# The last three microseconds of a decode block: the output in two transfers from two engines, and wd in parts of six, four and two chunks

## The chip, the cores and the metric

The kernel runs on one core of one Trainium2 chip. The metric is the device time of that core in microseconds (us), the median of several runs. The experiments ran on three chips of the same kind, each beside the kernel before on the same chip. Besides the time, each run has a profile of one execution. Where the profile's own views are too coarse, I read two more records from the same trace: the start of every DMA packet, and the moment of every semaphore increment by a DMA ("landing").

## The reference, cut to what matters

One token for each of four sequences passes through an attention block and a feed-forward block. Nearly all bytes are the key and value caches; the change concerns only the end, where the feed-forward block's down projection is multiplied and the result stored.

```python
def setup_inputs():
    B, Sq, D = 4, 1, 640
    Hq, Hkv, Sk, Dh = 32, 32, 4096, 192      # k_cache and v_cache: [4, 32, 4096, 192] bf16
    ...                                      # w_gate, w_up: [640, 1536]; w_down: [1536, 640]

def reference(A_x, A_k_cache, A_v_cache, A_wq, A_wo, B_x, B_w_gate, B_w_up, B_w_down):
    ...
    def _B_ref(x, w_gate, w_up, w_down):
        g = _silu(x @ w_gate)
        u = x @ w_up
        return (g * u) @ w_down

    x = A_x
    h = x + _A_ref(_layernorm(x, axis=-1), A_k_cache, A_v_cache, A_wq, A_wo)
    h2 = h + _B_ref(_layernorm(h, axis=-1), B_w_gate, B_w_up, B_w_down)
    return h2                                # [4, 1, 640] bf16: 5 KB
```

## The kernel before

All loads but that of the 5 KB input are issued by SyncE, in the order in which they are needed; w_down ("wd") is the last, in three parts. It is used as `CF` = 12 chunks of 128 rows. Each chunk is four matmuls, one for each quarter of the 640 columns, and a chunk waits for the part that holds it.

```python
    wd_land = {}
    for lo, hi in ((0, 6), (6, 11), (11, CF)):
        t = dma("sp", lambda e, lo=lo, hi=hi: e.dma_start(
            wdsb[:, lo:hi, :], wd[:, :].rearrange("(q c) n -> q c n", c=CF)[:, lo:hi, :]), sem(f"s_wd{lo}"), k_free)
        for c in range(lo, hi):
            wd_land[c] = t
    # ... attention, layer norm, gate and up projections ...
    for c in range(CF):
        for n in range(4):
            a = op("pe", lambda e, c=c, n=n: e.matmul(
                psH[32 * n:32 * n + 32, 0:DQ], lhsT=guT[:, c, :], rhs=wdsb[:, c, n * DQ:(n + 1) * DQ],
                start=False, stop=(c == CF - 1), skip_group_check=True), [gut, wd_land[c], ln2])
    a = op("dve", lambda e: e.tensor_copy(out=outsb[:, 0:DQ], in_=psH[:, 0:DQ]), [a])
    fin = dma("act", lambda e: e.dma_start(
        out[:, 0, :].rearrange("b (n d) -> n b d", n=4),
outsb[0:128:RB, 0:DQ]), S_out, [a])
```

The result lies on 16 of the 128 partitions: quarter n of the columns of sequence b is on partition 32n + 8b, 160 values of bf16 (320 bytes). The store therefore moves 16 rows of 320 bytes in a pattern of 4 x 4 rows. ScalarE issues it, waits for the semaphore `S_out`, and ends the program.

## Time and profile before

| | before |
|---|---|
| time, median of 3 runs before the prediction | 990.47 us (990.11 to 990.52) |
| span of the profiled execution | 988.4 us |
| mean DMA rate over the span | 429 GB/s |
| PE busy, DVE busy | 59%, 56% |
| last landing of wd | 985.08 us |
| start of the cast that produces the output | 985.79 us |
| start of the output's issue; its last landing | 986.14 us; 987.90 us |

From the page of before: the busy time of each engine, the rate in 40 slices, and the count of packets by size.

```profile
span 988.4 us, 9461 instructions
PE 580.1 (59%) x4409; PEld 129.6 (13%) x2941; DVE 552.5 (56%) x447; ACT 117.1 (12%) x376; POOL 3.6 (0%) x18
DMA  9999999999999999999999999999999999999997
GB/s 403 426 440 432 430 438 424 440 430 434 438 424 442 430 432 438 424 442 430 434 436 426 440 434 430 438 426 438 434 430 438 426 438 434 430 438 426 438 431 325
DMA packets 10571, 424.39 MB, mean 429 GB/s; under 512 B 1220, under 2 KB 1348, under 8 KB 1732
```

In 39 of 40 slices the DMA engines are at 90% or more. The loads bound the kernel, and only what follows the last load, in the last slice, can be shortened by a change at the end.

From the chain of work that ended last, its last three steps in order of time (start us, length, what; "issue" steps of 0.02 to 0.04 us between them left out):

```profile
946.58 38.12 DMA wd_sb<-in_B_w_down_dram
984.75 1.02 PE pb L573 x18
985.79 0.33 DVE gu L576
```

The first of them is the second part of wd, which landed at 946.58 + 38.12 = 984.70 us; the last six chunks and the cast follow from it. Here is the timeline of the end, without a line of weight loads (start us, length, engine, line, operation, out<-in, count, and in brackets the idle time before and what ended it):

```profile
982.93 0.99 PE L573 MATMUL pb<-wd_sb,guT 128*32 128x160 bf16 x24 [1.62 <-DVE guT L569]
984.74 0.67 PEld L573 LDWEIGHTS pb<-wd_sb,guT 128*32 128x32 bf16 x24 [1.15 <-DMA wd_sb<-in_B_w_down_dram]
984.75 0.99 PE L573 MATMUL pb<-wd_sb,guT 128*32 128x160 bf16 x24 [0.83 <-DMA wd_sb<-in_B_w_down_dram]
985.79 0.33 DVE L576 CAST gu<-pb 128x160 bf16<-128x160 f32 x1 [2.91 <-PE pb L573]
986.14 1.13 ACTq L577 DMA_DIRECT2D out_dram<-gu  x1
```

The first six chunks (24 matmuls) run as soon as their input is there. Then PE waits 0.83 us for the second part and runs the last six chunks without a break: the third part, one chunk, landed before its chunk's first matmul started at 985.38 us. After the cast, the issue on ScalarE is recorded with 1.13 us.

### The profile page before, as it was taken

Reading aid. Unit: us, or ns where it says so; the run is one execution under the profiler, and the core shown is the slowest. Engines: PE = TensorE matmul, PEld = TensorE weight load, DVE = VectorE, ACT = ScalarE, POOL = GpSimd, SP = SyncE. Lnnn points to the kernel's source line nnn. Section 1 sums busy time; section 2 is a strip of 40 time slices with the busy share of each in tenths; the row PEclk is TensorE's granted clock in tenths of the full one; section 3 lists DMA queues with packets and bytes.
Section 4 is the critical chain, followed back from the end, with each engine's and each line's share of the span. In section 5 each row is a group of like instructions: output and inputs, shape, how many; then the busy total and the mean of one; then the engine's idle time right before and its main releaser. Section 6 shows DMA issues by size and latency. Waiting matters only on the chain.

```text
span 988.4 us, 9461 instructions
## 1 busy us (share of the span) xinstructions
PE 580.1 (59%) x4409; PEld 129.6 (13%) x2941; DVE 552.5 (56%) x447; ACT 117.1 (12%) x376; POOL 3.6 (0%) x18
## 2 busy tenths in 40 slices
PE   1677555666555576555557755656665555765554
PEld 0011011110101111001111110111101011110023
DVE  1486555566645556664556665555666455566621
ACT  0311111110111110011111011111101111100120
POOL 1000000000000000000000000000000000000000
PEclk9898777887777888777788777788877778887775
DMA  9999999999999999999999999999999999999997
GB/s 403 426 440 432 430 438 424 440 430 434 438 424 442 430 432 438 424 442 430 434 436 426 440 434 430 438 426 438 434 430 438 426 438 434 430 438 426 438 431 325
DMA packets 10571, 424.39 MB, mean 429 GB/s; under 512 B 1220, under 2 KB 1348, under 8 KB 1732
## 3 DMA queue, kind: packets, MB, share of 16 engines
q1 hardware_dynamic: 10512, 424.28, 99.5%
q8 instruction: 5, 0.08, 0.0%
q10 hardware_dynamic: 52, 0.01, 0.0%
q14 instruction: 2, 0.02, 0.0%
HBM read 424.29 MB, written 0.01 MB: 429 GB/s over the span
## 4 chain that ended last, share of the span: by engine, by line
DMA 67%; PE 18%; DVE 12%; issue 1%; SPq 1%; DVEq 0%
DMA k<-in_A_k_cache_dram 63%; DVE prod L413 12%; PE pb L161 12%; PE pb L463 4%; DMA wd_sb<-in_B_w_down_dram 4%; PE pb L421 2%; SPq L366 0%; DVE sc L426 0%; PE pb L469 0%; DVEq L413 0%; PE pb L573 0%; SPq L386 0%; SPq L392 0%; PE pb L435 0%; SPq L331 0%
## 5 line engine op out<-in xcount | busy, mean ns | idle before, releaser
L413 DVE TENSOR_TENSOR prod<-k,qball 128x6144 f16<-128x6144 bf16 x128 | 426.3, 3352 | 220.7 <-DMA k<-in_A_k_cache_dram 220.7
L161 PE MATMUL pb<-prod,identH 128*128 128x512 f16 x1408 | 385.0, 430 | 0.0
L421 PE MATMUL pb<-prod,identH 128*128 128x512 f16 x128 | 57.9, 452 | 339.5 <-DVE prod L413 339.5
L426 DVE TENSOR_REDUCE sc<-pb 128x32 f32<-128x512 f32 x128 | 88.0, 688 | 107.6 <-PE pb L161 107.6
L478 ACT ACTIVATE otmp<-pb,minv 128x192 f32<-128x192 f32 x32 | 13.5, 421 | 650.8 <-PE pb L463 650.8
L421 PEld LDWEIGHTS pb<-prod,identH 128*128 128x128 f16 x128 | 13.2, 103 | 586.2 <-DVE prod L413 481.3
L463 PE MATMUL pb<-v,pbuf 128*8 128x384 bf16 x1984 | 86.0, 326 | 0.0
L454 ACT ACTIVATE pbuf<-sc,negM 32x128 bf16<-32x128 f32 x128 | 73.4, 574 | 4.9
L463 PEld LDWEIGHTS pb<-v,pbuf 128*8 128x8 bf16 x1984 | 45.4, 86 | 28.8
L482 DVE SCALAR_TENSOR_TENSOR orow<-pb,minv,otmp 128x192 f32<-128x192 f32 x32 | 13.4, 418 | 55.0 <-ACT otmp L478 55.0
L498 PEld LDWEIGHTS pb<-orow,here 128*128 128x128 f32 x256 | 33.5, 191 | 73.8 <-issue 71.1
L498 PE MATMUL pb<-orow,here 128*128 128x48 f32 x256 | 31.7, 267 | 1.1 <-DVE orow L482 1.1
L454 ACT ACTIVATION_READ_ACCUMULATOR pbuf<-sc,negM 32x1 f32 x128 | 31.8, 248 | 0.0
L448 ACT ACTIVATE negM<-pb 128x4 f32<-128x4 f32 x32 | 5.6, 174 | 160.9 <-PE pb L444 160.9
L469 PEld LDWEIGHTS pb<-lsb,headm 128*128 128x128 f32 x64 | 12.3, 194 | 74.8 <-issue 71.1
L444 PE MATMUL pb<-negMc,ones_row 1*128 1x4 f32 x64 | 12.2, 258 | 11.9 <-DVE negMc L439 11.9
L435 PE MATMUL pb<-identF,msb 128*1 128x128 f32 x64 | 12.1, 271 | 9.8 <-DVE msb L431 9.8
L439 DVE TENSOR_REDUCE negMc<-pb 1x4 f32<-1x128 f32 x32 | 8.9, 279 | 15.1 <-PE pb L435 15.1
L444 PEld LDWEIGHTS pb<-negMc,ones_row 1*128 1x128 f32 x64 | 9.4, 182 | 21.3 <-DVE negMc L439 21.3
L469 PE MATMUL pb<-lsb,headm 128*128 128x1 f32 x64 | 9.2, 213 | 2.7 <-ACT pbuf L454 2.7
L491 ACT ACTIVATE here<-place 128x131 f32 (+1 forms) x32 | 10.0, 312 | 0.9
L431 DVE TENSOR_REDUCE msb<-sc 128x1 f32<-128x128 f32 x32 | 9.2, 286 | 1.1
(65 smaller groups left out, 85.1 us busy)
## 6 DMA issues: line engine op xcount, KB each, us to landing
k<-in_A_k_cache_dram SPq DMA_DIRECT2D x32, 6144.0 KB, 39.5
v<-in_A_v_cache_dram SPq DMA_DIRECT2D x31, 6144.0 KB, 25.5
wq_sb<-in_A_wq_dram SPq DMA_DIRECT2D x1, 7680.0 KB, 21.4
k<-in_A_v_cache_dram SPq DMA_DIRECT2D x1, 6144.0 KB, 39.2
wo_sb<-in_A_wo_dram SPq DMA_DIRECT2D x1, 5760.0 KB, 24.9
wo_sb<-in_A_wo_dram SPq DMA_DIRECT2D x1, 1920.0 KB, 26.9
wg_sb<-in_B_w_gate_dram SPq DMA_DIRECT2D x1, 1920.0 KB, 31.1
wu_sb<-in_B_w_up_dram SPq DMA_DIRECT2D x1, 1152.0 KB, 33.4
```

The lines of the kernel that those rows point to most:

```text
L161: return e.add_instruction(mybir.InstMatmult(name=e.bass.get_next_instruction_name(), engine=mybir.EngineType.PE, start_tensor_calc=start, ...
L413: op("dve", lambda e: e.tensor_tensor(out=prod[BUF[k]][:, :, :], in0=kslot[u % 2][:, k * QT:(k + 1) * QT, :], in1=qball[:, bass.ds(u + pr. ...
L421: op("pe", lambda e, j=j: (e.matmul if j == 0 else partial(held_matmul, e))(psR[k][:, 0:QT * R], lhsT=identH[:, :], rhs=prod[BUF[k]][:, :, ...
L426: op("dve", lambda e: e.tensor_reduce(sc[u % 2][:, k * QT:(k + 1) * QT], psR[k][:, 0:QT * R].rearrange("q (t r) -> q t r", r=R), AX.X, ALU ...
L435: op("pe", lambda e: e.matmul(psS[0:1, XT], lhsT=msb[:, 0:1], rhs=identF[:, :], start=True, stop=True), [g("rmax", u), g("negM", u - 1), p ...
L444: op("pe", lambda e: e.matmul(psS[:, XB], lhsT=ones_row[0:1, :], rhs=negMc[0:1, :], start=True, stop=True), [g("hmax", u), g("negM", u - 1 ...
L454: op("act", lambda e, h=h, r=r: e.activation(out=pbuf[r, :, h], in_=sc[u % 2][r, :], func=ACTF.Exp, bias=negM[r, h:h + 1], scale=alpha, ac ...
L463: op("pe", lambda e, t=t, n=n: e.matmul(psO[32 * n:32 * n + 8, 0:2 * DH], lhsT=pbuf[:, t:t + 2, :].rearrange("q t m -> q (t m)"), rhs=vsrc ...
L469: op("pe", lambda e: e.matmul(psS[:, XL], lhsT=headm[:, :, :].rearrange("q r m -> q (r m)"), rhs=lsb[:, :], start=True, stop=True), [g("ex ...
L478: op("act", lambda e: e.activation(out=otmp[:, :], in_=psO[:, 0:DH], func=ACTF.Copy, scale=minv[:, 0:1]), [g("pv", u), g("minv", u), g("st ...
L482: op("dve", lambda e: e.scalar_tensor_tensor(out=orow[:, :], in0=psO[:, DH:2 * DH], scalar=minv[:, 1:2], in1=otmp[:, :], op0=ALU.mult, op1 ...
L498: op("pe", lambda e, i=i: e.matmul(psT[:, bass.ds(JW * at_unit(u)[0], JW)], lhsT=here[:, NI - 1 - i:NI - 1 - i + 128], rhs=orow[:, JW * i: ...
```

## The change

Its intent is twofold. The second part of wd gets smaller, so that it lands earlier, and the third larger. The output's 16 rows go out in two transfers of eight, issued side by side by SyncE and ScalarE, so that each engine has less to issue.

```diff
-    for lo, hi in ((0, 6), (6, 11), (11, CF)):
+    for lo, hi in ((0, 6), (6, 10), (10, CF)):
...
-    fin = dma("act", lambda e: e.dma_start(
-        out[:, 0, :].rearrange("b (n d) -> n b d", n=4),
-outsb[0:128:RB, 0:DQ]), S_out, [a])
+    fin = [dma(eng, lambda e, n=n: e.dma_start(
+        out[:, 0, n * DQ:(n + 2) * DQ].rearrange("b (n d) -> n b d", n=2),
+        outsb[32 * n:32 * n + 64:RB, 0:DQ]), S_out, [a]) for n, eng in ((0, "sp"), (2, "act"))]
...
-        pr.emit(block, "act", [fin])
+        pr.emit(block, "act", fin[-1:])
```

The last wait is for the second token, whose value on `S_out` counts both transfers, so the program still ends after both.

## The prediction

> **What bounds the kernel now.** The loads. The page's slices show the DMA engines at 90% or more in 39 of 40 slices (mean 429 GB/s), while PE is busy 59% and DVE 56% of the 988.4 us span. The chain that ended last gives DMA 67%. The change touches only the last 4 us.
>
> **The end, from the timeline.** The DMA traffic thins out from 982.8 us and ends at 984.6 (windows of 0.1 us: share 1.16 at 982.9, about 0.2 from 984.0, 0 after 984.7): a few engines finish about 1.5 us after the others. The down projection runs its first six chunks at 982.93 (0.99 us), waits 0.83 us for the second part of wd (issued 946.58, landed 38.12 us later, 984.70), and runs the last six from 984.75 in 0.99 us. The third part (160 KB) landed near 985.05, before its chunk was reached, so it held nothing up. Then come the cast (985.79, 0.33 us) and the output's issue on ScalarE (986.14, 1.13 us); the output's bytes move at 987.40 to 987.55; the span ends at 988.4.
>
> **Part one, wd in 6, 4, 2.** The second part ends one chunk earlier. A lagging engine moves its 10 KB of a chunk in about 0.38 us (27 GB/s, an estimate from the windows), so chunks 6 to 9 should start near 984.35, end by 985.0, and the last two wait briefly for the third part (985.05, unmoved) and run 0.33 us. The cast moves from 985.79 to about 985.5: 0.25 us won. Packets under 2 KB should fall from 1348 to 1220, as 128 pieces of 1280 B become 2560 B.
>
> **Part two, two output transfers.** "DMA: Bandwidth & Descriptors" of the Trainium skill (Issuing engines are not separate DMA queues) says that issuing from several engines saves only sequencer time. That is what matters here: the issue of 16 rows in a 4x4x160 pattern took 1.13 us, against 0.40 us for the input's 16 rows in one plain pattern. If the excess is per row (about 45 ns, an estimate), eight rows cost about 0.77 us on each engine, side by side. Against it: the same page (Why a DMA increments its semaphore by 16 and not by 1) says that a transfer uses a number of engines that divides its slowest dimension, so the pieces share two engines instead of four. The output occupies about 0.34 engine-us in the windows; doubled per engine this costs about 0.09 us. If the excess is a fixed cost of the pattern, nothing is won. Weighing both, 0.2 us won.
>
> PE and DVE instructions are unchanged in order and number, so the loop should not move.
>
> **Sum.** 990.47 - 0.25 - 0.2 = 990.0 us, 0.05% faster, all on the chain. The repeats span 0.4 us, so it may barely show. Range 989.4 to 990.6. Faster by over 2%: 0.003; within 2%: 0.994; slower by over 2%: 0.003.
>
> **What would show it.** Right: the last 24 matmuls split in 16 and 8, the 16 starting 0.3 to 0.4 us earlier after guT; a wait under 0.2 us before the last eight; the two issues at the same moment, each 0.7 to 0.9 us; cast's end to span's end (2.28 us now) about 2.1. Wrong: issues near 1.1 us each, or one delayed by the other; the third part landing later than 985.1.
>
> **What would make it wrong.** The imbalance of the DMA engines at the end may differ by 0.5 us between runs and swallow the gain. SyncE may react later than ScalarE. [...]

## The result, and the profile after

| | before | after |
|---|---|---|
| time, median of 6 runs | 990.52 us (990.11 to 990.92) | 990.43 us (990.17 to 990.64) |
| ratio | | 0.9999, 95% interval 0.9986 to 1.0012 |
| span of the profiled execution | 988.4 us | 988.4 us |

A ratio here and below is the mean time of one kernel's fast runs over the mean of the other's in the same rounds, so it is not quite the ratio of the medians quoted. The time is the same within noise, and the interval is 2.6 us wide. Both parts of the change are far below that, so the time alone cannot say what they did. The traces can: their durations at the end repeat to a few hundredths of a microsecond from run to run, as the table of the experiments will show.

The page and the end of the chain of after:

```profile
span 988.4 us, 9462 instructions
DMA packets 10571, 424.39 MB, mean 429 GB/s; under 512 B 1220, under 2 KB 1220, under 8 KB 1732
947.66 37.35 DMA wd_sb<-in_B_w_down_dram
985.06 0.48 PE pb L573 x6
985.57 0.33 DVE gu L576
```

The packets between 512 bytes and 2 KB are gone, as predicted (128 pieces of 1280 bytes became 2560 bytes). The chain now runs through the third part of wd, landed at 947.66 + 37.35 = 985.01 us, and the last eight matmuls after it (0.48 us). The timeline of after:

```profile
982.80 0.99 PE L573 MATMUL pb<-wd_sb,guT 128*32 128x160 bf16 x24 [1.65 <-DVE guT L569]
984.28 0.40 PEld L573 LDWEIGHTS pb<-wd_sb,guT 128*32 128x32 bf16 x16 [0.81 <-DMA wd_sb<-in_B_w_down_dram]
984.28 1.24 PE L573 MATMUL pb<-wd_sb,guT 128*32 128x160 bf16 x24 [0.49 <-DMA wd_sb<-in_B_w_down_dram]
985.06 0.14 PEld L573 LDWEIGHTS pb<-wd_sb,guT 128*32 128x32 bf16 x8 [0.38 <-DMA wd_sb<-in_B_w_down_dram]
985.57 0.33 DVE L576 CAST gu<-pb 128x160 bf16<-128x160 f32 x1 [2.86 <-PE pb L573]
985.92 0.68 SPq L577 DMA_DIRECT2D out_dram<-gu  x1
985.92 1.38 ACTq L577 DMA_DIRECT2D out_dram<-gu  x1
```

Two things are to be seen. The last six chunks start 0.47 us earlier than before (984.28 against 984.75), then stop in the middle: the weight loads idle 0.38 us and go on when the third part has landed. The cast starts 0.22 us earlier. And the two issues do start together, but they are not alike: SyncE's is recorded with 0.68 us, ScalarE's with 1.38 us, longer than the 1.13 us that ScalarE took for twice the rows.

The windows show when the output's bytes moved (stretch, its length, busy time of each engine, clock, DMA share, GB/s). Before:

```profile
987.10:987.30 0.20, 0.00 (x0) 0.00 (x0) 0.00 (x0) 0.00 (x0) 0.00 (x0) 0.50 0.00 0
987.30:987.43 0.13, 0.00 (x0) 0.00 (x0) 0.00 (x0) 0.00 (x0) 0.00 (x0) 0.50 0.00 0
987.43:987.60 0.17, 0.00 (x0) 0.00 (x0) 0.00 (x0) 0.00 (x0) 0.00 (x0) 0.50 0.13 30
```

After:

```profile
987.10:987.30 0.20, 0.00 (x0) 0.00 (x0) 0.00 (x0) 0.00 (x0) 0.00 (x0) 0.50 0.05 13
987.30:987.43 0.13, 0.00 (x0) 0.00 (x0) 0.00 (x0) 0.00 (x0) 0.00 (x0) 0.50 0.00 0
987.43:987.60 0.17, 0.00 (x0) 0.00 (x0) 0.00 (x0) 0.00 (x0) 0.00 (x0) 0.50 0.06 15
```

Half of the bytes now move earlier, but the other half moves when all of them moved before, although the cast was earlier by 0.22 us. The gain of wd seems to be given back by the store. By the records of packets and landings: before, the first packet started 1.29 us after the issue, and the last landing came 1.76 us after it. After, SyncE's first packet came at 1.27 us, ScalarE's at 1.54 us, and the last landing at 1.96 us. The load stream also ended 0.06 us earlier in this one profile (985.01 against 985.08, before rounding 985.014 and 985.075), which no part of the change needs to have caused.

So the question for the chip is whether the two halves cancel, and why ScalarE's half is late. My theory is that the two issues pass one after another through something they share. The rivals are that ScalarE by itself is slow with a half transfer; that the upper half of the partitions is slow; and, later, that the two transfers hinder each other on the DMA engines that they both use.

### The profile page after: what moved, and what is told of

It reads as the page before. It is cut to its first block, busy times and chain, and to the rows that moved or that the text cites. A ratio compares the mean times of both kernels' runs of the same rounds, so it can differ in the third digit from the quotient of the medians.

```text
span 988.4 us, 9462 instructions
## 1 busy us (share of the span) xinstructions
PE 581.5 (59%) x4409; PEld 128.6 (13%) x2941; DVE 552.6 (56%) x447; ACT 117.1 (12%) x376; POOL 3.6 (0%) x18
## 4 chain that ended last, share of the span: by engine, by line
DMA 67%; PE 18%; DVE 12%; issue 1%; SPq 1%; DVEq 0%
DMA k<-in_A_k_cache_dram 64%; DVE prod L413 12%; PE pb L161 11%; PE pb L463 4%; DMA wd_sb<-in_B_w_down_dram 4%; PE pb L421 2%; SPq L366 0%; DVE sc L426 0%; PE pb L469 0%; DVEq L413 0%; SPq L392 0%; SPq L386 0%; PE pb L573 0%; PE pb L435 0%; SPq L331 0%
## 5 line engine op out<-in xcount | busy, mean ns | idle before, releaser
L338 PE MATMUL pb<-wq_sb,lnT 128*32 128x384 bf16 x20 | 2.7, 520 | 12.1 <-DMA wq_sb<-in_A_wq_dram 12.1
```

## The experiments

### 1 and 2: one part of the change at a time

Run e1_wd_only has only this of the change:

```diff
-    for lo, hi in ((0, 6), (6, 11), (11, CF)):
+    for lo, hi in ((0, 6), (6, 10), (10, CF)):
```

> The change's first half alone: wd in parts of six, four and two chunks, output in one transfer from ScalarE. If the two halves cancel: the cast of the output starts near 985.5 us (985.79 before, 985.57 after), the single issue takes 1.13 us, cast's end to span's end stays at 2.28 us, and the span is 0.2 to 0.3 us shorter than before (988.1 to 988.2). If the wd parts gain nothing and the cast moved only because that run's load stream ended earlier: cast near 985.8, span 988.4.

Run e2_out_only has only the two output transfers, with wd as before:

```diff
-    fin = dma("act", ...16 rows...)
+    fin = [dma(eng, ...8 rows...) for n, eng in ((0, "sp"), (2, "act"))]
```

> The change's second half alone: output in two transfers, wd in six, five and one. If the two halves cancel: issues of about 0.68 us on SyncE and 1.38 us on ScalarE, cast's end to span's end about 2.5 us against 2.28 before, span 0.2 to 0.3 us longer than before (988.6 to 988.7). If the slow issue on ScalarE was chance: both issues 0.7 us and the span 0.2 us shorter.

By time: e1 990.16 us (990.00 to 990.73, ratio 0.9998, 0.9985 to 1.0012), e2 990.45 us (990.31 to 990.80, ratio 1.0000, 0.9987 to 1.0014), before 990.47 us in the same rounds. Neither is clear of noise. Their timelines are. e1:

```profile
984.34 1.23 PE L573 MATMUL pb<-wd_sb,guT 128*32 128x160 bf16 x24 [0.43 <-DMA wd_sb<-in_B_w_down_dram]
985.62 0.33 DVE L576 CAST gu<-pb 128x160 bf16<-128x160 f32 x1 [2.76 <-PE pb L573]
985.97 1.13 ACTq L577 DMA_DIRECT2D out_dram<-gu  x1
```

e2:

```profile
984.68 0.99 PE L573 MATMUL pb<-wd_sb,guT 128*32 128x160 bf16 x24 [0.82 <-DMA wd_sb<-in_B_w_down_dram]
985.72 0.33 DVE L576 CAST gu<-pb 128x160 bf16<-128x160 f32 x1 [2.92 <-PE pb L573]
986.08 0.69 SPq L577 DMA_DIRECT2D out_dram<-gu  x1
986.08 1.39 ACTq L577 DMA_DIRECT2D out_dram<-gu  x1
```

The end of the load stream moves from run to run. To be free of that, I measure from the last landing of wd. The next table has the kernels that end with one plain store or pair, those of later experiments included; times in us, from the records of the traces, rounded after subtraction where a column is a difference (so a sum of the rounded columns can be 0.01 off).

```
kernel            wd parts   output            last wd   landing  issue to   last wd landing
                                               landing   to cast  last land  to last output landing
before            6,5,1      one, ScalarE      985.08    0.71     1.76       2.83
e2_out_only       6,5,1      two               985.04    0.69     1.97       3.02
e1_wd_only        6,4,2      one, ScalarE      985.06    0.55     1.77       2.68
after             6,4,2      two               985.01    0.55     1.96       2.87
e12_after_again   6,4,2      two               985.06    0.56     1.96       2.87
e8_swap_halves    6,4,2      two, exchanged    985.42    0.56     1.98       2.89
e6_one_from_sp    6,4,2      one, SyncE        987.21    0.56     1.78       2.69
e9_warm           6,4,2      one, warmed       985.17    0.56     1.66       2.57
e10_best          6,4,1,1    one, warmed       985.39    0.42     1.66       2.44
```

The upper four rows are the two parts of the change with each other. wd alone gives 0.15 us (2.83 to 2.68). The two transfers alone cost 0.19 us (2.83 to 3.02). Together they make 2.87, which is 0.04 us more than before, just the sum. The whole effect of the change is this near cancellation. With parts of 6, 5 and 1 the cast waits for the second part, so the column "landing to cast" also carries the distance of the last two landings, 0.37 to 0.41 us: in the six traces with these parts it is 0.68 to 0.71 us, so wd's gain is 0.12 to 0.16 us. By issue to last landing alone the pair costs 0.20 to 0.22 us.

Why wd gave 0.15 us and not the predicted 0.25: the third part landed when it had been predicted to (985.01 to 985.06, predicted 985.05), but then eight matmuls remained. From that landing to the cast's start it took 0.55 us, where the prediction had allowed 0.45 (985.05 to 985.5). It had given these eight a third of the 0.99 us of 24, 0.33 us. Their step in the chain is 0.48 us: single matmuls are recorded with 0.31 to 0.34 us and overlap, so a short row of them takes more than its share of a long one.

### 3 and 4: the store 24 times

To see the cost of the pair in the time itself, the store was repeated 24 times, each waiting for the one before. The result stays right, as every store writes the same values.

```diff
+    fin = a
+    for i in range(24):
+        fin = whole("act", [fin])                       # e3_one_x24: 16 rows from ScalarE
```

> The output stored 24 times with the single transfer from ScalarE, each waiting for the one before, so that the disputed cost is counted 24 times. From the profile before, one store takes about 2.2 us (1.13 us issue, bytes 1.26 to 1.41 us after its start, the landing after that), so 23 more add about 50 us. It is the base for the next run.

```diff
+    fin = a
+    for i in range(24):
+        old = fin
+        part("sp", 0, [old])                            # e4_pair_x24: 8 rows each
+        fin = part("act", 2, [old])
```

> The same 24 times with the two transfers of eight rows, both waiting for both of the round before. If the pair costs 0.2 to 0.3 us more in every round: 5 to 7 us longer than the run with the single transfer. If only the first, cold round was slow: the same time or, with two issues of 0.68 us side by side, some 5 to 10 us shorter.

e3 took 1028.80 us (1028.65 to 1029.29), e4 1034.42 us (1034.00 to 1034.78), before 990.47 us. The pair costs (1034.42 - 1028.80) / 24 = 0.23 us per round on average, here clear of noise by time. My size for e3 was wrong: 23 more stores added 38.3 us, not 50. The reason is in the profile. Groups by tile (durations min/median/max ns, first and last start), e3:

```profile
L578 ACTq DMA_DIRECT2D out_dram<-gu x24: 543/544/1134, 986.1 to 1024.9; - x24
```

e4:

```profile
L578 SPq DMA_DIRECT2D out_dram<-gu x24: 497/510/682, 986.2 to 1029.9; - x24
L578 ACTq DMA_DIRECT2D out_dram<-gu x24: 518/518/1385, 986.2 to 1029.9; - x24
```

Only the first issue takes 1.13 us; the later ones take 0.54 us. Below, such a first store is called cold and the later ones warm. And in the pair ScalarE's later issues take 0.52 us, hardly less than for 16 rows and hardly more than SyncE's, yet every round is longer. So the recorded length of a warm issue does not show the loss. What shows it are the packets: in warm rounds of e4, SyncE's first packet came 1.15 us after its issue and ScalarE's 1.42 or 1.50 us after, against 1.19 us for the single store of e3.

### 5, 7 and 8: which of the theories

Run e5_forms_x8 has eleven forms of the store in a row, eight rounds each, every round waiting for the one before. The first round of each form is left out below.

```diff
+    for i in range(8):
+        old = fin
+        fin = dma("act", ...16 rows...)       # then the same loop with: 16 rows from SyncE; each half from
+                                              # ScalarE, each from SyncE; the pair; the pair exchanged;
+                                              # both halves from SyncE; both from ScalarE; 16 rows again
```

> Eleven forms of the store, eight times each, one waiting for the other, so all but the first are warm: whole from ScalarE; whole from SyncE; each half alone from each engine; the pair; the pair with the halves exchanged; both halves from SyncE; both from ScalarE; whole again. In the warm rounds so far the single store's first packet moves 1.19 us after its issue starts, and in the pair SyncE's at 1.15 and ScalarE's at 1.42 to 1.50. Theory 1, the two issues pass one after another through something they share: half from ScalarE alone has its first packet at 1.15 to 1.20 us, and in both pairs one engine's packets come 0.27 to 0.36 us after the other's. Theory 2, ScalarE alone is slow with this half transfer: first packet at 1.42 to 1.50 us without SyncE beside it. Theory 3, the upper half of the partitions is slow: late from either engine, and in the exchanged pair it is SyncE that is late.

Run e7_act_half_first sends ScalarE's half first, in the cold state of the real kernel, and SyncE's half only when it has landed:

```diff
-    ... S_out, [a]) for n, eng in ((0, "sp"), (2, "act"))]
+    fin = a
+    for n, eng in ((2, "act"), (0, "sp")):
+        fin = dma(eng, ...8 rows..., S_out, [fin])
```

> After's two transfers one after another: ScalarE's half first and alone, SyncE's when it has landed. Theory 1 (shared): the first issue on ScalarE takes at most 1.13 us, the time of the whole transfer, and its first packet moves 1.1 to 1.3 us after its start. Theory 2 (ScalarE slow with a half transfer): 1.38 us and first packet at 1.54 us, as beside SyncE. The kernel as a whole is about 1.5 us longer than after.

Run e8_swap_halves exchanges the halves:

```diff
-    ... for n, eng in ((0, "sp"), (2, "act"))]
+    ... for n, eng in ((2, "sp"), (0, "act"))]
```

> After with the halves exchanged: SyncE sends the upper one, ScalarE the lower. Theories 1 and 2: nothing changes, 0.68 us on SyncE and 1.38 us on ScalarE, span as after. Theory 3 (the upper half is slow): SyncE's issue and packets are the late ones.

The results, from the records of the traces, in us after the issue's start (the first round of each form is left out, the two cold looks apart):

```
                                        issue recorded   first packet   round
e5  16 rows, ScalarE alone              0.54             1.19           1.68 to 1.69
e5  16 rows, SyncE alone                0.52 to 0.55     1.16 to 1.20   1.66 to 1.68
e5  8 rows (either half), ScalarE alone 0.52             1.16 to 1.17   1.60 to 1.61
e5  8 rows (either half), SyncE alone   0.50 to 0.52     1.14 to 1.16   1.58 to 1.60
e5  pair: SyncE lower                   0.50 to 0.51     1.14 to 1.15
          ScalarE upper                 0.52             1.41 to 1.50   1.85 to 1.94
e5  pair: SyncE upper                   0.50 to 0.51     1.14 to 1.15
          ScalarE lower                 0.52             1.42 to 1.50   1.86 to 1.94
e5  both halves from SyncE              0.50, 0.51       1.14, 1.15     2.12 to 2.14
e5  both halves from ScalarE            0.52, 0.52       1.16, 1.16     2.15 to 2.16
e5  16 rows, ScalarE again              0.54 to 0.56     1.19 to 1.20   1.68 to 1.69
e7  8 rows, ScalarE alone, cold         1.13             1.29
e8  SyncE upper, cold                   0.69             1.28
    ScalarE lower, cold                 1.39             1.55
```

The two single looks took 992.23 us (e7) and 990.59 us (e8).

ScalarE alone sends a half on time, warm (1.16 us) and cold (1.29 us), so it is not slow by itself. Exchanged halves change nothing, so it is not the place of the data. ScalarE's half is late only beside SyncE's, by 0.25 to 0.34 us. Of the three theories that were put to these runs, only the shared passage stands. Two halves from one engine, whose issues start 0.54 us apart, do not delay each other (1.14 and 1.15 us), but a round of them takes 2.12 to 2.16 us. Two engines are thus 0.2 to 0.3 us quicker than one for two transfers; it is against one transfer that they lose.

The recorded length of an issue can now be read better. A warm store that nothing delays has its first packet 0.64 to 0.65 us after the recorded end of its issue, so the 0.03 us more that an issue of 16 rows takes on ScalarE go with packets 0.03 us later. Only ScalarE's cold store differs: there 0.16 us lie between the two, alone as beside SyncE, and the delay is inside the record (1.13 us alone, 1.38 to 1.39 us beside SyncE). On SyncE's cold store it is 0.59 to 0.60 us.

The table also tells how little there was to win. A half alone takes 1.61 us warm, the whole 1.68 us. Even two issues that did not disturb each other would have saved 0.07 us, by this estimate. Of it 1.16 us (eight rows) and 1.19 us (sixteen) pass before any byte moves. And the cold half on ScalarE took 1.13 us to issue, just as the cold whole: the excess over the input's 0.40 us was not per row.

### 6: the single transfer from SyncE

Against e1:

```diff
-    fin = dma("act", ...16 rows...)
+    fin = dma("sp", ...16 rows...)
```

> wd in six, four and two, and the output in one transfer, but from SyncE. If SyncE handles a first issue quicker than ScalarE: issue of 0.7 us against 1.13, and a store of about 1.65 to 1.7 us from issue to last landing, against 1.76 for the single one from ScalarE and 1.97 for the pair: span about 988.1. If only the number of rows set the issue time: 1.13 us and span 988.2, as with wd alone changed.

SyncE's issue is recorded with 0.70 us as expected, but the store took 1.78 us from issue to last landing, not 1.65 to 1.70, the same as from ScalarE with its 1.13 us. First packets came at 1.30 us from either. The recorded length of a cold issue on ScalarE is thus a poor measure of what it costs: 0.43 us less on SyncE brought nothing. The time was 990.26 us (990.04 to 992.16; before 990.62, 990.22 to 993.25), ratio 0.9995 (0.9981 to 1.0008), no difference. (The profiled execution of this run lost 2 us earlier, in the load stream, where the last landing is at 987.21 us; the row in the table is free of that.)

### 11: what the partner must be

Run e11_partner_x8 puts other transfers of SyncE beside ScalarE's half, to tell a shared passage ahead of the DMA engines from a collision on them.

```diff
+    for i in range(8):
+        old = fin
+        dma("sp", ...one row | four rows | a load of 16 plain rows..., S_out, [old])   # each also alone
+        fin = dma("act", ...8 rows..., S_out, [old])
```

> What must SyncE send for ScalarE's half to be late? Eight warm rounds each of: the pair as it is; one row alone; one row beside ScalarE's half; four rows alone; four rows beside it; a load of 16 plain rows alone; that load beside it. ScalarE's half alone has its first packet at 1.16 us, beside SyncE's half at 1.41 to 1.50. Theory 1a, the issues share something before the DMA engines: late by 0.2 to 0.35 us whatever the partner's size. Theory 1b, they wait for each other on the two DMA engines that both use: with one row (one engine) as partner, half of ScalarE's packets are on time at 1.16, and the delay shrinks with the partner's packets per engine, from four in the pair to one.

In the column "alone" the first two rounds of each form are left out, as they were up to 0.1 us slower.

```
first packet, us after the issue        SyncE alone   SyncE beside    ScalarE beside
one row                                 0.70          0.70 to 0.71    1.16 to 1.17
load of 16 plain rows                   0.91 to 0.92  0.92 to 0.93    1.16 to 1.17, once 1.23
four rows                               1.22          1.52 to 1.53    1.16 to 1.17
eight rows, rounds 3 to 8               (e5) 1.14     1.14 to 1.16    1.42 to 1.50
eight rows, rounds 1 and 2              to 1.16       1.56, 1.44      1.28, 1.16
```

Neither of the two forms that I had written down is right as it stands. The delay does not come whatever the partner is: beside one row or a plain load, whose packets start well before 1.16 us, ScalarE is on time. But it does not shrink with the partner's packets either. Four rows, ready later than ScalarE's half (1.22 against 1.16), let ScalarE pass on time and are themselves late by 0.30 us. In the first two rounds of this run even the plain pair came in the other order, and SyncE was the late one. All this fits one reading: whoever is ready first goes first, and the other is delayed by about 0.3 us, if the two would be ready at nearly the same time (within 0.02 to 0.06 us of each other here; a partner 0.24 us ahead, the load, did no harm). ("Ready" is the time of the first packet when alone.) That nearness in time decides is argued, not isolated: the two partners that did no harm also differ in form and size from those that did, and no run had the same partner at several distances.

The four rows also speak against the collision on the DMA engines. A transfer ends with one 4-byte packet for each engine that it uses, by the rule cited under "Two engines instead of four" below; the packets do not name their engine. There are four of them in the whole store and in the four rows, two in a half. So the four rows use four engines and ScalarE's half two. On at least two of the four nothing of ScalarE's half was in the way, yet all four rows' packets were late. The plain load speaks against it too: in six of its eight rounds it still had packets starting up to 1.22 to 1.29 us, and ScalarE's began at 1.16 us amid them, but for the one round at 1.23. One round of the four rows, records of the trace (time, queue 10 is ScalarE's and queue 1 SyncE's):

```
1041.186 to 1041.263   q10   8 packets of 320 bytes, the last at 1041.246; 2 of 4 bytes
1041.543               q1    320 bytes
1041.557               q1    320 bytes
1041.577               q1    320 bytes
1041.608               q1    320 bytes; 4 packets of 4 bytes between 1041.557 and 1041.623
```

Queue 1 begins 0.28 us after queue 10 started its last packet, and no packet of any queue moved in between. The wait lies ahead of the packets, after the issue's start. Whether it is still before the DMA engines or in them ahead of the first packet, and what the shared thing is, no view shows, and it stays open.

### 9, 10 and 12: a version that keeps the gain

Two costs had shown up that can be had without a second transfer: the first store's 0.1 us on the way to its first packet (1.29 us cold, 1.19 warm), and the eight matmuls after the last landing. Run e9_warm has wd in 6, 4, 2 and sends, some 28 us before the last store, another store of constants in the same form to the output. It is overwritten later, after a wait.

```diff
+    warm = dma("act", lambda e: e.dma_start(
+        out[:, 0, :].rearrange("b (n d) -> n b d", n=4),
+        sel[:, :, :].rearrange("q b i -> q (b i)")[0:128:RB, 0:DQ]), S_out, [ksel])
...
-outsb[0:128:RB, 0:DQ]), S_out, [a])
+outsb[0:128:RB, 0:DQ]), S_out, [a, warm])
```

> wd in six, four and two, one store from ScalarE, and some 25 us before it a store of constants in the same form from ScalarE (out is overwritten later, after a wait). If the 1.13 us are a cost of the first store on that engine, the final issue takes 0.54 to 0.57 us, its first packet comes at 1.19 to 1.21 us instead of 1.29, and issue to last landing is 1.66 to 1.70 us instead of 1.76; last wd landing to cast's start stays at 0.56 us. If 25 us of other work undo the warming: 1.13 us and 1.76 us again.

Run e10_best has this too, and wd in four parts:

```diff
-    for lo, hi in ((0, 6), (6, 10), (10, CF)):
+    for lo, hi in ((0, 6), (6, 10), (10, 11), (11, CF)):
```

> As the warmed kernel, with wd in six, four, one and one. The last landing then holds up four matmuls instead of eight: last landing to cast's start about 0.46 us, against 0.56 with six, four, two and 0.69 with six, five, one. With the warm store: last landing to the span's end about 0.3 us shorter than before. By time 990.1 to 990.2 against 990.5 of before, not clear of noise. If a fourth transfer delays the last landing itself, nothing is left of the 0.1 us.

Run e12_after_again is the changed kernel, unedited.

> After once more, on the chip of the last two kernels, for a comparison with them: median within 0.3 us of before, SyncE's issue 0.68 to 0.69 us, ScalarE's 1.38 to 1.39 us, last landing of wd to cast's start 0.56 us, issue to last landing 1.96 to 1.97 us.

Timeline of e10:

```profile
984.64 1.12 PE L576 MATMUL pb<-wd_sb,guT 128*32 128x160 bf16 x24 [0.46 <-DMA wd_sb<-in_B_w_down_dram]
985.80 0.33 DVE L579 CAST gu<-pb 128x160 bf16<-128x160 f32 x1 [2.67 <-PE pb L576]
986.16 0.54 ACTq L580 DMA_DIRECT2D out_dram<-gu  x1
```

The issue is recorded with 0.54 us, 28 us after the first. From issue to last landing it is 1.66 us in both, 0.10 us less than before, and with four parts only 0.42 us lie between the last landing of wd and the cast. From the last landing of wd to that of the output, e10 takes 2.44 us, against 2.83 of before and 2.87 of after. In this one profile wd's last landing was itself late, at 985.39 us; since already the first part was late (983.03 against 982.66 to 982.82 in the others at 985.2 or less), I take it for the stream's variation. The landings speak for that: from the first part's to the last's it took 2.35 us here, and 2.30 to 2.35 us in the other eight traces of the table.

By time, in the same rounds: before 990.34 us (989.99 to 990.79), e9 990.14 us (ratio 0.9998, 0.9985 to 1.0012), e10 990.08 us (0.9998, 0.9985 to 1.0012), after 990.64 us (1.0002, 0.9989 to 1.0016). The medians stand in the order of the traces' sums, but no ratio is clear of noise: 0.4 us in 990 is 0.04%, and the interval is 0.27% wide.

## Why the prediction was right or wrong

- **What bounds the kernel, and that the time stays within 2%:** right. 990.43 us lies in the range of 989.4 to 990.6, beside a forecast of 990.0. But the forecast gain of 0.45 us was not there: the trace has a loss of 0.04 us in the end's durations. Right time and wrong account are compatible here because every term is smaller than the noise; that the time fell into the range says nothing for the terms.
- **wd in 6, 4, 2 ("the cast moves from 985.79 to about 985.5: 0.25 us won"):** right mechanism, size off. The second part landed at 984.24 (predicted start of its chunks 984.35, measured 984.28), the third at 985.01 (predicted 985.05). The mis-sized term is what follows the third landing: predicted 0.45 us up to the cast, measured 0.55, as the last eight matmuls took 0.48 us and not 0.33. The wait before them was predicted under 0.2 us; the weight loads idled 0.38 us. Worth 0.15 us by itself.
- **Two transfers ("if the excess is per row ... eight rows cost about 0.77 us on each engine, side by side"; "0.2 us won"):** wrong, and this is the step that failed. The excess was not per row: a cold half on ScalarE took the same 1.13 us as the whole, and a warm whole took 0.54 us. Nor did its length count: 0.70 us on SyncE gave the same store time as 1.13 us on ScalarE. And the two did not go out side by side: one passes first, the other's packets come about 0.3 us late. Instead of 0.2 us won, about 0.2 us were lost. The prediction had named "one delayed by the other" as a sign of being wrong.
- **Two engines instead of four, "about 0.09 us":** the sign of it is in the trace, as each half ended with two 4-byte packets and the whole with four, so the Trainium skill's rule (DMA: Bandwidth & Descriptors, section Why a DMA increments its semaphore by 16 and not by 1: the number of engines divides the slowest dimension, and each of them counts up the semaphore at its end) agrees with this. In e11 a single row ended with one such packet and the 16 plain rows with sixteen. As a cost it was not put to the test: in after, the second half's packets began 0.19 us after the first half's had ended, so they never met on an engine.
- **What the Trainium skill says of issuing from several engines** (the same page, section Issuing engines are not separate DMA queues: it "will only save the time on the sequencer it takes to initiate the DMA"): I took this as a promise against one transfer, and there nothing was saved: the second transfer's packets came 0.25 to 0.34 us late. Against both halves from one engine, e5 agrees in sign: 1.85 to 1.94 us a round instead of 2.12 to 2.16, where the engine's second issue had started 0.54 us after its first.
- **"PE and DVE instructions are unchanged ... the loop should not move":** right; PE has 4409 and DVE 447 instructions in both, and the span is 988.4 us in both.

## What to carry to other kernels

A small store at the very end of a kernel is nearly all latency: of the 1.76 us here, 1.29 us pass before the first packet, and halving the rows saved 0.07 us warm, so splitting it over two engines could hardly win and lost 0.2 us because the two did not go out side by side. Judge such a step from its issue's start to its last landing, not from the recorded length of the issue alone, and repeat it some 24 times where the kernel's noise hides it. For the last load of a kernel, look at how much work is left after its last landing: with parts of 6, 5 and 1 chunks, 6, 4 and 2, and 6, 4, 1 and 1, the cast started 0.71, 0.55 and 0.42 us after it.

## What the Trainium skill lacked or had wrong

- DMA: Bandwidth & Descriptors, section Issuing engines are not separate DMA queues: it doesn't say that two DMAs issued at the same moment by SyncE and ScalarE can delay each other before the second one's packets start. The page's section Rules for kernel authors does advise against two transfers to disjoint partition halves ("Don't bother — they serialize"), but puts it down to the DMA engines that both halves share. Here the second one's first packet came 0.25 to 0.34 us late (1.41 to 1.50 us against 1.16), whichever engine was second, and not when the partner was ready much earlier (first packet at 0.70 or 0.92 us).
- The same page, sections Specifications and Latency and other measured facts: it gives about 0.6 us as first-byte latency for transfers from the sync and scalar engines, but not from where it counts. Here the figure fits the recorded end of the issue: 0.64 to 0.65 us for warm stores of 4, 8 or 16 rows that nothing delayed, 0.60 to 0.62 us for a plain load of 16 rows, 0.48 us for a single row. From the issue's start it was 1.14 to 1.22, 0.92 and 0.70 us.
- The same page, section Anatomy of one DMA: for transfers issued by GpSimd it puts most of the fixed 2 us down to the write's receipt; it has no such split for the other engines, and no run here has a GpSimd transfer. In the 1.76 us store from ScalarE, 0.34 us lie between the end of the last packet and the last landing, and 1.29 us before the first packet.
- No page that I read has the cost of the first store on an engine: ScalarE's first such issue is recorded with 1.13 us and later ones with 0.54 us, SyncE's with 0.68 to 0.72 and 0.50 to 0.55 us, of which only about 0.10 us reach the first packet. It is not the engine's first DMA of any kind: SyncE had issued all the loads before, and ScalarE's load of the input, its first, was recorded with 0.40 us.
